# The first FFN matmul of segments 1 to 3 in 64-row tiles on a doubled input, with four general PSUM banks and a new timetable

## The chip, the core and the metric

The kernel runs on one core of a Trainium2 chip. Its engines each work through a queue of their own, in order, and wait for one another by semaphores: TensorE (PE, with PEld for its weight loads), VectorE (DVE), ScalarE (ACT), GpSimd (POOL) and SyncE (SP), whose queue issues nearly all DMAs. The metric is the device time of one execution in microseconds (us). The profile is taken in one further execution.

## The reference, cut to what matters

Two layers on a sequence of 2048 rows of 576 features, in bf16. The first is an attention with a memory, over four segments of 512 rows, the second a feed-forward network (FFN) of 4608 hidden features. Both have a layer norm ahead and a residual behind.

```python
# attention, per segment s of 4 (512 rows), 32 heads of 18
p = softmax(q @ k.T * scale + causal_mask);  a_dot = p @ v
a_mem = (phi(q) @ M) / (phi(q) @ z + 1e-6)      # M, z: sums over the segments ahead
o = g * a_mem + (1 - g) * a_dot
M += phi(k).T @ v;  z += phi(k).sum()
# the whole
h  = x + o @ wo                                  # q, k, v from layernorm(x)
h2 = h + gelu(layernorm(h) @ w1 + b1) @ w2 + b2  # w1: 576 x 4608, w2: 4608 x 576
```

## The kernel before, in words

The rows go through the core in four segments of 512 (s = 0 to 3, `L = 512`), each of four tiles of 128 rows (`TPS = 4`). The stages have letters, and the rows of the timetable begin with them: X (layer norm and transpose of the input), P (projections to q, k, v), M (the memory), A (attention), B (output projection, residual, second layer norm, transpose), C (first FFN matmul, called F1, with its Gelu) and D (second FFN matmul, F2, residual and output).

**Order.** Nothing is ordered by loops alone. `build()` lists operations (`add`), each with a cost per engine, the operations that it comes after, the buffers that it takes (`acq`) and those that it uses. The table `TIMETABLE` gives each one a letter for its engine (p, a, d, g, s) and a number, and `schedule()` sorts all operations by that number. So the order on every engine's queue is fixed in the table, ahead of the run. `schedule()` also picks for each buffer the slot that it expects to be free first; that is all that the costs are used for. The waits are set by the tile framework from reads and writes.

**PSUM.** There are eight banks of 512 fp32 columns. Three are general (`c_s`, tiles ps_c). One (`ox`) takes the value products of attention. The other four hold the scores (`st`, one buffer of four banks, in use from the first score step on), and after the last exp they become `ps_l`, four banks for F1 of segments 2 and 3 (`to_late`), which also uses `ox` then (`late_s`, five banks).

**F1 of segments 0 and 1** (L1224 and the lines around it). The normed rows lie transposed in `x2T`: features on the partitions, in five blocks of 128 (`KT = 5`), rows along the free axis. The 576 features fill four blocks and half of the fifth; the fifth block has a row of ones behind them, the 65th row (`KTAIL = 65`), which multiplies the bias b1. One block of 128 hidden features over 512 rows is five matmuls into one bank, and there are 36 such blocks (`NF = 36`); segment 0 does them in two halves of 256 rows. ACT or DVE copy the bank to `hT` (L597, L601), and in three batches a segment ACT does the Gelu in place (L1241), between the exps of attention; for each batch it loads the Gelu's table and then that of exp again. F1 of segment 1 stands among the score steps of attention of segments 2 and 3.

**F1 of segments 2 and 3** (L1188, `TILED = 2`) runs in 64-row tiles: TensorE works as two halves, rows 0 to 63 and 64 to 127, which each take a matmul at the same time, into banks of their own. The fifth block's upper half holds the last 64 features once more (`tail`, a copy on POOL, L1129), so that they can be had on either half. A group of four blocks is done in four phases of 5, 5, 4 and 4 pairs. In phases 0 and 1 a block takes its even chunks of 64 features on the lower half while another takes its odd chunks on the upper; in phases 2 and 3 the banks pass to the other half. Ahead of each passing stands a `mark`, a tiny memset on POOL (L1197) that waits for the phase that used the bank last. ACT does the Gelu with the bias straight from the bank (gelu1, L1208). This F1 can begin only after the last exp, when the score banks are free.

**x2T.** `flip` (L588) is a DMA transpose, issued on SP, from the rows in DRAM (`x2d`). The buffers xT (two, for the input of the projections) and x2T (one) are separate tiles; segments 1 and 3 put their transposed rows into an xT slot, segments 0 and 2 into the x2T slot. Segment 0's first half is transposed by TensorE.

**Weights.** A load on SP (L581) brings the weights of four blocks (640 KB) into one of three buffers `w1g`.

**Other lines.** L755 projections, L920 and L1049 scores (32-row tiles) of segment 0 and of the others, L924 and L1053 their exp, L945 and L1075 value products (32-column tiles in segments 1 to 3), L1027 the memory product ("mem") on exp of q (L1017, "eg"), L857 M, L1275 F2 (chunks of six matmuls of 288 columns), L1123 and L1287 the residuals.

Of the kernel before, what the change touches and what calls it, by code (L numbers as in the profile page):

```python
# [24 lines left out]
    "A00T": "p 166",  # L25
    "A00comb": "d 131 152",
    "A00copy": "d 171",
    "A00exp": "a 81 106",
    "A00mask": "g 95 103 133 128",
    "A00perm": "g 160",  # L30
    "A00st0": "p 76 96",
    "A00val": "p 105 129 145 147",
    "A01T": "p 224",
    "A01comb": "d 186 211",
    "A01copy": "d 227",
    "A01exp": "a 139 123 168 191",
    "A01mask": "g150 g165 d192 g190",
    "A01perm": "g 217",
    "A01st0": "p 136 118 151 187",
    "A01val": "p 163 179 169 167 197 199 205 208",  # L40
    "A02comb": "d 432 471",
    "A02dma": "s 487",
    "A02exp": "a 342 369 355 387 451 427",
    "A02mask": "g367 g351 d411 g398",
    "A02perm": "g 480",
    "A02st0": "p 339 364 353 382 446 408",
    "A02val": "p 378 394 380 390 393 410 436 437 468 463 457 449",
    "A03comb": "d 301 371",
    "A03dma": "s 460",
    "A03exp": "a 218 267 249 234 282 329 302 314",  # L50
    "A03flip": "s 503",
    "A03mask": "g 236 230 292 300",
    "A03opad": "g 585",
    "A03oxz": "d 484",
    "A03perm": "g 374",
    "A03st0": "p 214 264 246 231 279 325 295 309",
    "A03val": "p 248 260 285 281 263 266 258 257 313 316 366 341 336 315 334 333",
    "A0flip": "s 91 86 113 104 178 170 220 213",
    "A1comb": "d 579 624 663 719 757 794 829 847",
    "A1comb2": "g589 g636 d688 g722 d760 g803 g839 g851",  # L60
    "A1eg": "a 461 475 614 648 580 730 726 681",
    "A1exp": "a 469 499 483 550 515 570 587 604 620 634 657 671 693 707 734 721 763 776 792 808",
    "A1flip": "s 416 422 496 529 453 558 664 641",
    "A1mask": "g476 g507 d512 g516 g535 g565 g532 g527 g606 g610 g596 g615 g656 g650 g645 g660 d676 g680 d694 g701 g738 g735 d748 d746 g727 d782 d781 g789 "
        "g784 g820 g816 d838",
    "A1mem": "p 517 542 649 706 602 775 795 723",
    "A1memT": "d 521 549 655 709 607 779 815 737",
    "A1memfin": "d 525 631 677 712 704 798 835 828",
    "A1oT": "d 669 802 812 855 859",
    "A1pq": "d 500 492 643 697 584 755 765 710",  # L70
    "A1rg": "g 456 454 581 601 510 733 740 685",
    "A1st": "p 465 495 478 528 511 567 582 599 616 628 652 668 682 702 728 718 753 773 788 805",
    "A1val": "p 546 578 621 665 714 750 801 842",
    "A1valT": "d 561 598 659 689 744 790 809 845",
    "A2comb": "d 917 947 1003 1032 1059 1092 1128 1161",
    "A2comb2": "g922 g975 g1007 g1034 d1062 g1097 g1131 g1166",
    "A2eg": "a 804 874 878 968 1008 952 1056 1012",
    "A2exp": "a 849 823 869 883 899 915 944 930 961 973 987 1014 1028 1002 1044 1060 1074 1096 1087 1114",
    "A2flip": "s 767 800 824 787 898 868 1026 943",
    "A2mask": "g864 g830 g833 g880 g875 g893 d912 g908 g928 g953 d963 d937 d990 d969 d982 d986 d1000 g1023 g1020 d1036 d1046 g1029 g1061 g1052 g1069 g1103 "  # L80
        "g1081 d1106 g1129 d1120 g1127 g1121",
    "A2mem": "p 857 914 965 1009 1048 994 1072 1107",
    "A2memT": "d 863 927 974 1016 1050 997 1076 1110",
    "A2memfin": "d 865 971 1005 1021 1053 1030 1098 1112",
    "A2oT": "d 1070 1082 1155 1175 1179",
    "A2pq": "d 850 884 959 993 1033 983 1066 1088",
    "A2rg": "g 836 853 918 924 988 979 1064 1085",
    "A2st": "p 844 821 866 877 894 910 940 926 957 970 984 1010 1022 999 1038 1054 1071 1093 1083 1108",
    "A2val": "p 892 923 966 995 1040 1067 1111 1133",
    "A2valT": "d 902 931 980 1015 1045 1086 1116 1152",  # L90
    "A3comb": "d 1245 1273 1310 1362 1372 1399 1433 1443",
    "A3comb2": "g1261 g1276 g1329 d1366 g1379 g1403 d1437 d1444",
    "A3eg": "a 1119 1080 1229 1295 1268 1323 1383 1345",
    "A3exp": "a 1126 1139 1171 1186 1236 1257 1272 1219 1286 1301 1331 1313 1342 1351 1360 1374 1387 1397 1412 1426",
    "A3flip": "s 1041 989 1109 1115 1235 1164 1330 1284",
    "A3mask": "g1143 g1146 g1189 d1193 g1181 d1248 g1243 d1247 d1283 d1279 g1280 g1290 g1302 g1305 d1314 g1315 d1340 d1337 g1324 d1346 g1347 g1361 g1378 "
        "g1370 g1413 g1393 d1402 d1414 g1407 d1430 g1434 d1436",
    "A3mem": "p 1206 1228 1262 1316 1289 1380 1390 1416",
    "A3memT": "d 1210 1231 1265 1353 1303 1382 1405 1420",
    "A3memfin": "d 1259 1237 1288 1354 1306 1392 1424 1422",  # L100
    "A3oT": "d 1325 1455 1451 1445 1447",
    "A3pq": "d 1137 1144 1241 1308 1275 1376 1388 1350",
    "A3rg": "g 1100 1058 1140 1234 1253 1287 1384 1312",
    "A3st": "p 1122 1136 1162 1182 1230 1251 1270 1207 1282 1297 1326 1309 1339 1348 1357 1371 1385 1394 1408 1423",
    "A3val": "p 1209 1252 1294 1321 1349 1381 1421 1439",
    "A3valT": "d 1239 1269 1298 1334 1369 1395 1427 1441",
    "B00Po": "p 189 194",
    "B00T": "p 254",
    "B00apply": "d 232",
    "B00copy": "d 261",  # L110
    "B00dma": "s 143 524",
    "B00hadd": "d 196 200",
    "B00rstd": "g 223",
    "B00stats": "d 203",
    "B01Po": "p 233 237",
    "B01T": "p 262",
    "B01apply": "d 256",
    "B01copy": "d 265",
    "B01dma": "s 193 537",
    "B01hadd": "d 238 241",  # L120
    "B01rstd": "g 253",
    "B01stats": "d 244",
    "B02Po": "p 560 562",
    "B02apply": "d 609",
    "B02dma": "s 450 785 613",
    "B02hadd": "d 566 569",
    "B02rstd": "g 577",
    "B02stats": "d 572",
    "B03Po": "p 551 573",
    "B03apply": "d 627",  # L130
    "B03dma": "s 326 810 632",
    "B03flip": "s 651",
    "B03hadd": "d 556 576",
    "B03rstd": "g 622",
    "B03stats": "d 617",
    "B1Po": "p 897 901 867 881 872 873 933 938",
    "B1apply": "d 954 934 909 955",
    "B1dma": "s 886 951 956 818 996 936 807 887 913 905 962 960",
    "B1flip": "s 977",
    "B1hadd": "d 904 906 871 888 876 882 939 941",  # L140
    "B1rstd": "g 932 911 896 950",
    "B1stats": "d 920 895 891 945",
# [147 lines left out]
    "omg": "g 83",  # L290
    "ones": "a 278 338",
    "tri": "g 50",
    "warm": "p 5 11 18 23",
    "x1": "a 1",
}

# [1149 lines left out]
```

## Time and profile before

| what | value |
|---|---|
| time, median of 3 runs | 464.19 us (462.29 to 464.24) |
| the profiled execution: time | 463.85 us |
| the profiled execution: span, first to last instruction | 462.1 us |
| granted TensorE clock, mean | 0.996 |
| busy: PE, PEld, DVE, ACT, POOL | 451.1, 290.2, 288.7, 297.0, 143.3 us |
| F1 of segment 1 (L1224, 128x512) | 172 matmuls recorded, 41.2 us |
| F1 of segments 2 and 3 (L1188) | 324 pairs, from 309.0 to 426.3 us |
| F2 (L1275) | 1152 matmuls, 158.4 us |
| DMA | 78.10 MB, 169 GB/s in the mean |

How to read it: a group's row has its line, engine, operation and tile, then the busy time and mean duration in ns, then the engine's idle time ahead of it and what ended that. Matmuls overlap, so their mean duration is longer than the distance from one to the next; the timeline's starts give the distance. Some matmul records are missing, a few per cent. In a window's row, the first two numbers are the stretch and its length.

### The profile page before, as it was taken

The numbers are of one execution on the slowest core, as the hardware profiler recorded it, in microseconds if no ns is written. First come the engines' busy times: TensorE is split into PE (matmuls) and PEld (weight loads), VectorE is DVE, ScalarE is ACT, GpSimd is POOL, SyncE is SP. The second block draws the span as 40 slices with busy tenths as digits, with TensorE's granted clock in tenths as the row PEclk, the third lists the DMA queues.
The fourth block names the chain that finished last, engine by engine and source line by source line (L and its number), as shares of the span: only waits on it lengthen the run. The fifth ranks groups of instructions, "written<-read, shape, count | busy, mean of one in ns | idle before, by whom it ended". The sixth has DMA issues, their size and how long they took to land.

```text
span 462.1 us, 11032 instructions
## 1 busy us (share of the span) xinstructions
PE 451.1 (98%) x4569; PEld 290.2 (63%) x4577; DVE 288.7 (62%) x664; ACT 297.0 (64%) x283; POOL 143.3 (31%) x250
## 2 busy tenths in 40 slices
PE   8988999999999999999999999999999999999997
PEld 4766877866677776663344666554456774445775
DVE  6879978899987699889977887893211210000111
ACT  4877889999869787777899988744644004452100
POOL 4655415253513245445352244640001000001000
PEclk9989999999999999999999999999999999999999
DMA  7799789998798985555655125275650443351020
GB/s 242 221 270 208 227 278 293 230 264 235 224 238 280 326 218 147 160 119 128 198 167 147 39 64 146 70 192 165 199 205 16 112 165 112 129 177 43 8 75 22
DMA packets 75827, 78.10 MB, mean 169 GB/s; under 512 B 52992, under 2 KB 62976, under 8 KB 75776
## 3 DMA queue, kind: packets, MB, share of 16 engines
q1 hardware_dynamic: 75632, 77.24, 59.4%
q8 instruction: 36, 0.59, 0.5%
q10 hardware_dynamic: 144, 0.15, 0.1%
q14 instruction: 15, 0.12, 0.1%
HBM read 45.38 MB, written 19.53 MB: 140 GB/s over the span
## 4 chain that ended last, share of the span: by engine, by line
PE 81%; DVE 8%; ACT 4%; DMA 3%; SPq 2%; issue 1%; POOL 0%; DVEq 0%; ACTq 0%
PE ps_c L1275 28%; PE ps_c L1224 15%; PE ps_c L755 12%; PE ps_l L1188 11%; PE st L1049 4%; PE ox L1188 3%; PE ox L1075 3%; ACT pt L1053 2%; SPq L588 2%; ACT hT L1241 1%; PE ox L945 1%; PE ps_c L1027 1%; DMA xT<-xnd 1%; PE pr L766 1%; DMA qkd<-qk_pad 1%
## 5 line engine op out<-in xcount | busy, mean ns | idle before, releaser
L1275 PEld LDWEIGHTS <-hT 128*128 128x128 bf16 x1152 | 109.6, 98 | 37.8 <-issue 10.3
L1053 ACT ACTIVATE pt<-st 128x2048 bf16<-128x2048 f32 x60 | 112.7, 1878 | 30.4 <-PE st L1049 24.5
L1208 ACT ACTIVATE hT<-ps_l,b_col 128x512 bf16<-128x512 f32 x57 | 36.4, 687 | 66.7 <-PE ps_l L1188 64.4
L1275 PE MATMUL ps_c<-w,hT 128*128 128x288 bf16 x576 | 79.3, 287 | 0.0
L1275 PE MATMUL ps_c<-w_lo,hT 128*128 128x288 bf16 x576 | 79.1, 287 | 0.0
L1224 PEld LDWEIGHTS <-w1g 128*128 128x128 bf16 (+1 forms) x540 | 51.1, 97 | 26.1 <-issue 2.7
L755 PE MATMUL ps_c<-hT,xT 128*128 128x288 bf16 (+1 forms) x440 | 63.7, 290 | 1.9 <-DVE h L1123 1.1
L1064 POOL TENSOR_SCALAR_AFFINE_SELECT pt<-pt 128x512 bf16<-128x512 bf16 x63 | 42.6, 687 | 66.5 <-ACT pt L1053 66.4
L1287 DVE TENSOR_TENSOR ot<-ps_c,hc 128x288 bf16<-128x288 f32 x32 | 14.4, 451 | 75.0 <-PE ps_c L1275 46.4
L1188 PEld LDWEIGHTS <-w1g 64*128 64x128 bf16 x648 | 31.2, 94 | 37.9 <-issue 4.2
L755 PEld LDWEIGHTS <-xT 128*128 128x128 bf16 (+1 forms) x440 | 40.4, 98 | 15.2 <-issue 3.9
L601 DVE CAST hT<-ps_c 128x512 bf16<-128x512 f32 x51 | 34.7, 684 | 13.9 <-PE ps_c L1224 13.5
L1224 PE MATMUL ps_c<-x2T,w1g 128*128 128x256 bf16 (+1 forms) x360 | 43.2, 273 | 0.0
L924 ACT ACTIVATE pt<-st 128x2048 bf16<-128x2048 f32 x20 | 37.6, 1880 | 7.4 <-PE st L920 7.3
L1224 PE MATMUL ps_c<-xT,w1g 128*128 128x512 bf16 (+1 forms) x172 | 41.2, 380 | 0.4
L1188 PE MATMUL ps_l<-xT,w1g 64*128 64x512 bf16 x261 | 36.5, 377 | 0.3 <-ACT hT L1208 0.3
L1188 PE MATMUL ps_l<-x2T,w1g 64*128 64x512 bf16 x252 | 36.5, 377 | 0.0
L1197 POOL MEMSET mark<- 1x1 f32 x36 | 3.2, 88 | 99.1 <-PE ps_l L1188 85.5
L1241 ACT ACTIVATE hT<-hT 128x4608 bf16<-128x4608 bf16 (+2 forms) x7 | 32.1, 4592 | 0.1
L676 POOL TENSOR_TENSOR ln<-ln,mhalf 128x1 f32<-128x1 f32 x32 | 18.3, 576 | 37.4 <-DVE ln L673 37.3
L1123 DVE TENSOR_TENSOR h<-ps_c,xb 128x288 f32<-128x288 f32 x32 | 14.1, 452 | 24.6 <-PE ps_c L755 24.4
L1091 POOL TENSOR_TENSOR o_nat<-t,t 128x288 bf16<-128x288 f32 x18 | 16.9, 937 | 31.1 <-DVE t L1088 18.7
(116 smaller groups left out, 612.7 us busy)
## 6 DMA issues: line engine op xcount, KB each, us to landing
w1g<-in_B_w_dram SPq DMA_DIRECT2D x24, 640.0 KB, 4.7
w1g<-in_B_w1d_dram SPq DMA_DIRECT2D x18, 640.0 KB, 4.3
qkd<-qk_pad SPq DMA_DIRECT2D x15, 512.0 KB, 3.6
hd<-h SPq DMA_DIRECT2D x16, 288.0 KB, 3.3
hc<-hd SPq DMA_DIRECT2D x16, 288.0 KB, 3.2
w_lo<-in_B_w_dram SPq DMA_DIRECT2D x3, 864.0 KB, 5.2
w<-in_B_w_dram SPq DMA_DIRECT2D x3, 864.0 KB, 8.1
xb<-in_A_x_dram SPq DMA_DIRECT2D x16, 144.0 KB, 3.9
```

What stands on the lines that cost most here:

```text
L601: VEC[e].tensor_copy(out=dst(), in_=src())
L676: nc.gpsimd.tensor_tensor(out=sm.t[:, 15:16], in0=sm.t[:, 14:15], in1=mhalf[:], op=ALU.pow)
L755: nc.tensor.matmul(out=c.t[:, 0:HALF], lhsT=xTb.t[0:kk, k, ts], rhs=wt[0:kk, hf, k, :], start=(k == 0), stop=(k == 4))
L924: ex = add(ps, {"act": 1.88}, lambda e, st=st, pt=pt: nc.scalar.activation(out=pt.t[:], in_=st.t[:], func=ACT.Exp, scale=scale), [sc], pt, ...
L1049: nc.tensor.matmul(out=st.t[:, i, off:off + n_], lhsT=qk[rows, 1, kt * P:(kt + 1) * P], rhs=qk[rows, 0, kt * P:L], start=True, stop=True, ...
L1053: ex = add(ps, {"act": 1.88}, lambda e, st=st, pt=pt: nc.scalar.activation(out=pt.t[:], in_=st.t[:], func=ACT.Exp, scale=scale), [sc], pt, ...
L1064: nc.gpsimd.affine_select(out=blk, in_=blk, pattern=[[0, 4], [1, P]], compare_op=ALU.is_ge, fill=0.0, base=0, channel_multiplier=-1)
L1188: i = nc.tensor.matmul(out=cc[w].t[:], lhsT=w1.t[rows, ch // 2, w * P:(w + 1) * P], rhs=x2T[s].t[rows, ch // 2, :], start=ph < 2 and n == ...
L1208: ready_f[f] = [add(pf + 0.0001 * ph - 12, {"act": 0.68}, lambda e, f=f, w=w, cc=cc: nc.scalar.activation(out=hT[:, :, f, :], in_=cc[w].t[ ...
L1224: nc.tensor.matmul(out=c.t[:, u * n_:(u + 1) * n_], lhsT=w1.t[0:kk, k, j * P:(j + 1) * P], rhs=x2T[s].t[0:kk, k, ts], start=(k == 0), stop ...
L1241: ge = add(2.9 if half is None else GE_PRIO[half], {"act": (0.40 if half is None else 0.20) * (f1 - f0) + 0.25}, lambda e, f0=f0, f1=f1, h ...
L1275: nc.tensor.matmul(out=c.t[:, 0:HALF], lhsT=hT[:, tl // 2, f, (tl % 2) * P:(tl % 2 + 1) * P], rhs=w2_c[ch][:, f - ch * WCH, hf * HALF:(hf ...
```

## The change

- **Doubled input.** The tiles xT (two slots) and x2T become one tile `xreg`. For segments 1 to 3 its first nine blocks of 128 partitions are one buffer, `xd_s`, with nine blocks of two chunks each: the lower half holds the chunks 0 2 4 6 8 1 3 5 7, the upper half 1 3 5 7 0 2 4 6 8. Two flips fill it: the first as before (five blocks; the tail's 64 columns are now the first 64 features), the second four blocks from column 64 on. The first flip comes after all projections, since xT lies under it. There is one such buffer for three segments.
- **F1 of segments 1 to 3** does two blocks side by side: nine steps, each with a matmul on the lower half for one block and one on the upper half for the other. No bank passes from one half to the other, and the marks are gone. The weights are laid out to match (`by_pair`, 2304 columns a group in place of 2560) and are used for segment 1 too.
- **Segment 1** has no row of ones any more; the bias is added at the eviction (ACT Identity with a bias, or DVE add of a column). Its Gelu batches are 16, 14 and 6 blocks (15, 15 and 6 before). Segments 2 and 3 keep the Gelu from the bank.
- **Banks.** `ox` joins the general banks: four `c_s`, used for value products too; the late banks are four in place of five. The memset of ox is gone; the warm-up matmuls use general banks.
- **Planner.** Several costs are higher (flips, DVE operations); a flip's cost and size too.
- **Timetable.** Every row is new. A few are shown.

```diff
-    "A0flip": "s 91 86 113 104 178 170 220 213",
+    "A0flip": "s 96 85 127 119 184 192 202 231",
-    "B2flip": "s 1418",
+    "B2flip": "s 1360 1404",
-    "B3flip": "s 1618",
+    "B3flip": "s 1573 1584",
-    "C3F1": "p 1647 1648 1650 1652 1657 1660 1662 1664 1670 1672 1674 1676 1681 1684 1686 1688 1695 1696 1698 1700 1709 1712 1714 1716 1722 1727 1729 1731 "
-        "1754 1755 1757 1760 1736 1737 1741 1744",
+    "C3F1": "p 1612 1606 1620 1615 1627 1623 1630 1634 1641 1637 1648 1644 1655 1651 1658 1661 1667 1664",
...
-    BATCHES = (15, 30, 36)
-    TILED = 2
+    BATCHES = (16, 30, 36)
+    ND = 9
+    TILED = 1
+    DIRECT = 2
...
-    xT_s = slots(2, [P, KT, L], "xT")
-    x2_s = slots(1, [P, KT, L], "x2T")
+    xreg = const.tile([P, 3, KT, L], BF16, name="xreg")
+    xT_s = Slots([xreg[:, j, :, :] for j in range(2)])
+    x2_s = Slots([xreg[:, 2, :, :]])
+    xd_s = Slots([xreg[:].rearrange("p j k t -> p (j k) t")[:, 0:ND, :]])
...
-    ox_s = Slots([psum.tile([P, 512], F32, name="ox")])
-    c_s = slots(3, [P, 512], "ps_c", F32, psum)
+    c_s = slots(4, [P, 512], "ps_c", F32, psum)
...
-    late_s = Slots([None] * 4 + ox_s.tiles)
+    late_s = Slots([None] * 4)
...
-            x2T[s] = Buf(xT_s if s % 2 else x2_s)
+            x2T[s] = Buf(xd_s if s else x2_s)
...
                 if s >= TILED:
-                    ap = add(p0, {"pool": 0.2}, lambda e, xn2=xn2: nc.gpsimd.tensor_copy(out=xn2.t[:, D:XW], in_=xn2.t[:, D - 64:D]), [ap], None, [xn2],
+                    ap = add(p0, {"pool": 0.29}, lambda e, xn2=xn2: nc.gpsimd.tensor_copy(out=xn2.t[:, D:XW], in_=xn2.t[:, 0:64]), [ap] + first_ln, None, [xn2],
                              name="tail")
...
-                x2_ok[s].append(flip(prio, lambda: x2T[s].t[:], lambda: x2d[s][:, :], 520e3, w_, acq=x2T[s], cost=3.0))
+                x2_ok[s].append(flip(prio, lambda: x2T[s].t[:, 0:KT, :], lambda: x2d[s][:, :], 520e3, w_ + p3_done, acq=x2T[s], cost=3.0))
+                x2_ok[s].append(flip(prio, lambda: x2T[s].t[:, KT:ND, :], lambda: x2d[s][:, 64:D], 420e3, [x2_ok[s][0]], use=[x2T[s]], cost=2.4))
...
-                    if s >= TILED:
-
-                        cc = [Buf(late_s) for _ in range(4)]
-                        last, prev, phases, fences = {}, None, [], []
-                        pf = prh + 0.001 * (NF // 4 - fg)
-                        for ph in range(4):
...
+                    for q in (1, 0) if s >= TILED else ():
+                        f = fg * 4 + 2 * q
+                        cc = [Buf(c_s if s < DIRECT else late_s) for _ in range(2)]
+                        pf = prh + 0.001 * (NF - f)
+
+                        def fn(e, w1=w1, cc=cc, q=q):
+                            if s >= DIRECT:
+                                to_late()
+                            wv = w1.t[:].rearrange("p k f -> p (k f)")[:, 0:ND * 2 * P].rearrange("p (k q m) -> p k q m", q=2, m=P)
+                            for k in range(ND):
+                                for w in range(2):
+                                    rows = slice(64 * w, 64 * w + 64)
+                                    nc.tensor.matmul(out=cc[w].t[:], lhsT=wv[rows, k, q, :], rhs=x2T[s].t[rows, k, :], start=(k == 0), stop=(k == ND - 1))
+                        free = [o for w in range(2) for o in f2_chunks.get((s - 1, f + w), [])]
+                        a = add(pf, {"pe": 1.94}, fn, [la] + x2_in + free + (scores_done if s >= DIRECT else []), cc, [w1, x2T[s]], table="rows64", name="F1")
...
+                            def evict(e, f=f, w=w, cc=cc):
+                                dst, src, b = hT[:, :, f + w, :], cc[w].t[:].rearrange("p (h t) -> p h t", h=2), b1_col[:, f + w:f + w + 1]
+                                if e == "act":
+                                    nc.scalar.activation(out=dst, in_=src, func=ACT.Identity, bias=b)
+                                else:
+                                    nc.vector.tensor_scalar(out=dst, in0=src, scalar1=b, scalar2=None, op0=ALU.add)
+                            pend.append(add(pf - 16, {"act": 0.61, "dve": 0.69}, evict, [a, b1_ok], None, [cc[w]], name="copy"))
...
-                ox[g] = Buf(ox_s)
+                ox[g] = Buf(c_s)
...
+    def by_pair(w):
+        c = w.reshape(9, 64, 9, 2, 2, 128)
+        return np.concatenate([c[order, :, :, :, h].transpose(2, 1, 0, 3, 4) for h, order in enumerate(
+            ([0, 2, 4, 6, 8, 1, 3, 5, 7], [1, 3, 5, 7, 0, 2, 4, 6, 8]))], axis=1).reshape(9 * 128, 9 * 256)
...
-        B_w1d=by_group(blocks(w1, w1[512:576])),
+        B_w1d=by_pair(w1),
```

## The prediction

> **What bounds the kernel now.** I read the page's busy times first, then its 40 slices, then the windows by stage, the waits of TensorE, and the timeline where the first FFN matmul (F1) runs.
>
> ```profile
> span 462.1 us, 11032 instructions
> PE 451.1 (98%) x4569; PEld 290.2 (63%) x4577; DVE 288.7 (62%) x664; ACT 297.0 (64%) x283; POOL 143.3 (31%) x250
> PE   8988999999999999999999999999999999999997
> PEclk9989999999999999999999999999999999999999
> ...
> L1275 PE MATMUL ps_c<-w,hT 128*128 128x288 bf16 x576 | 79.3, 287 | 0.0
> L1208 ACT ACTIVATE hT<-ps_l,b_col 128x512 bf16<-128x512 f32 x57 | 36.4, 687 | 66.7 <-PE ps_l L1188 64.4
> ```
> TensorE (PE) is busy in every slice, and its clock is lower in one place only. F1's Gelu (L1208) waits 64 us for TensorE; nothing like that stands on the other side. After 50 us TensorE's waits on other engines add up to 2.1 us:
>
> ```profile
> PE ps_c L1027 <- DVE e L1021: 0.7, 2, 0.5
> PE st L1049 <- ACT pt L1053: 0.5, 2, 0.3
> PE ps_c L755 <- DVE oT L1100: 0.4, 1, 0.4
> PE ps_l L1188 <- ACT hT L1208: 0.3, 1, 0.3
> ```
> So from 50 us on the end is set by how many steps TensorE has to make. Two windows show where this is least sure: the start, and segment 3's attention, where ScalarE (ACT) is as full as TensorE.
>
> ```profile
> 28.00:32.00 4.00, 2.45 (x26) 1.57 (x27) 3.33 (x9) 1.83 (x6) 2.57 (x4) 0.79 1.07 314
> 32.00:36.00 4.00, 4.00 (x70) 3.17 (x69) 2.27 (x10) 2.93 (x5) 2.91 (x6) 0.79 1.16 283
> 205.00:309.00 104.00, 102.43 (x896) 56.22 (x905) 88.44 (x175) 87.10 (x57) 46.34 (x63) 1.00 0.45 125
> 245.00:265.00 20.00, 19.68 (x151) 11.72 (x152) 15.97 (x36) 19.52 (x12) 5.16 (x9) 1.00 0.30 86
> ```
> Columns: stretch, length, busy PE, PEld, DVE, ACT, POOL, granted clock, DMA share, GB/s. ACT is busy 19.52 of 20 us between 245 and 265.
>
> Prices of TensorE's steps come from the timeline (start, duration), from one start to the next:
>
> ```profile
> 234.07 7.75 PE L1224 MATMUL ps_c<-xT,w1g 128*128 128x512 bf16 x34
> 241.75 0.40 PE L1049 MATMUL st<-qk 32*128 32x256 bf16 x8
> 242.08 5.59 PE L1224 MATMUL ps_c<-xT,w1g 128*128 128x512 bf16 x24
> 247.60 0.40 PE L1049 MATMUL st<-qk 32*128 32x512 bf16 x4
> ...
> 375.42 1.63 PE L1275 MATMUL ps_c<-w_lo,hT 128*128 128x288 bf16 x12
> 376.89 1.64 PE L1275 MATMUL ps_c<-w,hT 128*128 128x288 bf16 x12
> ...
> 389.48 0.91 PE L1275 MATMUL ps_c<-w_lo,hT 128*128 128x288 bf16 x6
> 390.32 4.06 PE L1188 MATMUL ps_l<-xT,w1g 64*128 64x512 bf16 x36
> 394.32 0.91 PE L1275 MATMUL ps_c<-w,hT 128*128 128x288 bf16 x6
> ```
> Full-height F1: 35 matmuls (one record is missing) take 7.68 us and 25 take 5.52 us, so ten take 2.16: 0.216 each. Twelve F2 matmuls take 1.47, so a chunk of six 0.735. One chunk and 18 pairs of 64-row matmuls take 394.32 - 389.48 = 4.84. A pair at the full-height step of 0.216 makes 18 x 0.216 = 3.89; 4.84 - 0.735 - 3.89 = 0.22 is left for two changes of tile mode (128 rows to 64 and back): 0.11 each.
>
> **The change, part by part.** The sum is made against the profiled execution: 462.1 span, 463.85 time, 0.34 under the median of the three runs (464.19). Orders are those in which both kernels' instructions stand on each engine.
>
> *F1 of segment 1.* Now 36 blocks of 5 full-height matmuls, 180 x 0.216 = 38.9. After: 18 pairs of blocks of 9 steps, 162 x 0.216 = 35.0. TensorE: -3.9. Both halves of a step have the arrangement of L1188 (rows 0 to 63 and 64 to 127, a bank each). F1 of segments 2 and 3 has 162 steps before and after: nothing.
>
> The Trainium skill, "TensorEngine Tiling (Array Packing)", section "Instruction Overhead", speaks against this: it gives each matmul about 60 cycles of overhead, and segment 1 issues 324 instead of 180. Worked out from that page, an estimate, 144 x 25 ns = 3.6 us would eat this term and the forecast would be about 462.5. The row above has 36 matmuls in 18 steps of full-height length, so the row decides.
>
> *Changes of tile mode.* The orders have 221 before, 199 after: from segment 2's first F1 on 34 and 6 (16 of its 18 pairs, and all of segment 3's, now stand back to back), ahead of it 187 and 193, since segment 1's F1 has left the full mode. -22 x 0.11 = -2.4.
>
> *Segment 3's attention.* In the timeline a score step's exp starts 0.53 after the step (233.74, 234.27) and takes 1.88, and the scores have one buffer: the next step can start 2.43 after the last one. I filled the 19 gaps of the new order with rows: score step 0.33, F2 chunk 0.735, F1 pair 1.94, value product 0.55, memory product 0.12, 0.2 for changes of mode. Six gaps hold too little: a value and a memory product alone (short by 1.2), two chunks (0.4), two chunks and one or two memory products (0.3 and 0.2), one chunk with a value and a memory product (0.5, twice): 3.1. The old order gives 0.5 in the same way, which is what L1049 waited. Given back: +2.6. Behind a waiting score step stand the F2 chunks, which cannot pass it. Bounds: 0 (the exps still idle 24.5 us for scores over all segments) and +5.0, if the eight gaps that hold 2.5 to 2.75, and so just enough, are short by 0.3 each, half an exp of q (0.63, L1017; seven stand among these exps).
>
> *The start.* Before, TensorE waits 0.57 and 1.40 for flipped queries (L920), 0.58 for xT, 1.11 for h, and runs at 0.79 for 8 us, which is 1.7 us lost. After, the first two flips are issued ahead of a store of xn that they stood behind, two more half projections (0.62 each) stand ahead of the score step that waited first, and segment 0's memory product ahead of the other. That covers the 2.0; new are waits of values for masks and of a projection for its evacuated transpose, some 0.8 by the rows. I take -1.2. Bounds: -3.7 (2.0 and the half-speed stretch, 1.7) and +2.0 (a second such stretch and 0.3).
>
> The Trainium skill, "TensorE: Matmul & The Clock Gate", Part 1, says that the clock is halved after an idle window of about 3.4 us that runs free of the kernel. The two rows at 0.79 agree in size (1.7 us lost of 3.4); by the rule a stretch can come or go by phase alone, so the start could be worth 0 or -2.9 with the same order. The sum does not use it.
>
> *The doubled input.* Three more flips, of 4 blocks of 128 rows. A flip of 5 blocks holds SP 2.8 to 3.8 and lands 5 us after issue (L588, x2T and xT from x2d), so a second adds some 2.4 on SP's queue and 5 to readiness. There is one doubled buffer for three segments: a flip now waits for the last F1 of the segment ahead, and for the last projection of segment 3 (over by 130 us). What hides it: between the last F1 of segment 1 and the first of segment 2 stand some 40 F2 chunks (29 us), between those of 2 and 3 there are 48 (35 us). Behind the second flip on SP stand an output store, residual and weight loads, none needed within 10 us. Cost 0; without that cover about 10 us each. The added tail copy in segment 1 (POOL, 0.24, 4 of them) stands ahead of the same flip: 0.
>
> *Evictions.* In segment 1 the bias moves from the matmul's 65th row into 36 evictions, 25 on DVE and 11 on ACT. With a pointer operand ACT takes 0.687 (L1208) against 0.585 (L597), DVE 0.506 against 0.454 on 288 columns (L599, L601): 1.1 us on ACT, about 2.3 on DVE (0.052 scaled to 512 columns, 25 times), beside TensorE. DVE has 15 us free in 205 to 309. Cost 0 to 0.3, taken 0.
>
> *Banks, marks, loads.* F1 pairs take two of four banks. In segments 2 and 3 the two Gelus of a pair take 0.69 + 0.58 and the pair that runs meanwhile 1.94: not waited for. The 36 marks on POOL (L1197) and the memset of ox go: 0.2 us of waits, taken as 0. A weight group lasts 2 x 1.94 = 3.9 instead of 4.84; with three buffers the load is issued 7.8 ahead of use and lands in 4.3 (median), 6.6 at worst: 0.
>
> **Sum:** -3.9 - 2.4 + 2.6 - 1.2 = -4.9. 463.85 - 4.9 = 458.95; I say 459.0.
>
> **The rivals.**
> 1. *The start also loses its half-speed stretch:* waits 2.0 and clock 1.7 gone: -3.9 - 2.4 + 2.6 - 3.7 = -7.4, 456.4. For: fewer of the known waits meet in one place. Against: DMA is at 1.07 to 1.39 of its share there and every landing can slip.
> 2. *No measurable change:* attention gives back its upper bound and the start nothing: -3.9 - 2.4 + 5.0 = -1.3, 462.6. For: ACT at 29.0 of 30 us from 232 to 262. Against: 17 us of ACT's time are free in 205 to 309.
> 3. *Slower: ScalarE sets the pace of segment 3's attention.* Place: its score steps; price: an eviction or exp of about 0.6 inside the cycle of every one of 20 steps, +12.4 in place of 2.6: -3.9 - 2.4 + 12.4 - 1.2 = +4.9, 468.8. It decides from 0.5 us per step (9.8 cancel the rest plus 2.3). For: two Gelu batches (14 and 6 blocks; one of 15 takes 6.6) with their table loads (1.28 each) stand among the exps. Against: the old order has three there, and the new one only 2 evictions and 7 exps of q beside the 20 exps.
> 4. *The pairs do not run side by side in segment 1:* 324 x 0.216 = 70, some 490. L1188 excludes it but for a fault in the arrangement.
>
> **How the numbers follow.** Half a per cent is 2.3 us, about what a measurement can tell from no change. Forecast (457 to 461.5) 0.61, rival 1 0.17, rival 2 0.12, rival 3 0.09, rival 4 0.01. Faster: 0.61 + 0.17 = 0.78; same 0.12; slower 0.10. Of the bounds, all at once on the good side give 463.85 - 3.9 - 2.4 - 3.7 = 453.9, on the bad side 463.85 - 3.9 - 2.4 + 5.0 + 2.0 + 0.3 = 464.9; both need several to meet. 455.0 to 463.5 holds the forecast, most of rivals 1 and 2, and leaves out about 0.16. The forecast's own range is 457 to 461.5.
>
> **What would show it.** Right: F1 of segment 1 in pairs at 0.216 a step; from segment 2's first F1 to the end 3 us less (28 changes of mode); L1049 waiting for ACT about 3 us instead of 0.5; fewer waits of L920 for qkd. Wrong: TensorE waiting for a doubled flip or for weights ahead of F1; banks waited for in the back-to-back F1; a second stretch of low clock; the score steps of segment 3 at 2.4 us or more apart throughout with TensorE idle between.

## The result, and the profile after

| | before | after |
|---|---|---|
| median | 463.61 us (462.29 to 464.24, 4 runs) | 458.13 us (457.47 to 458.45, 4 runs) |
| profiled execution: time, span | 463.85, 462.1 us | 457.92, 456.2 us |
| granted TensorE clock in it | 0.996 | 1.000 |

The ratio is 0.988, with a 95% interval of 0.986 to 0.991: 5.5 us faster. 459.0 was predicted, 0.9 more than the median.

The page after, its busy times, two of its slices and the groups of F1 and of the evictions:

```profile
span 456.2 us, 11278 instructions
...
PE 443.6 (97%) x4721; PEld 290.2 (64%) x4721; DVE 282.5 (62%) x653; ACT 300.8 (66%) x285; POOL 148.6 (33%) x226
...
PE   7988999999999999999999999999999999999997
...
PEclk9999999999999999999999999999999999999999
...
L1192 ACT ACTIVATE hT<-ps_l,b_col 128x512 bf16<-128x512 f32 x72 | 45.2, 684 | 70.7 <-PE ps_l L1187 70.7
...
L1187 PE MATMUL ps_l<-xreg,w1g 64*128 64x512 bf16 x648 | 70.5, 376 | 0.0
...
L1187 PE MATMUL ps_c<-xreg,w1g 64*128 64x512 bf16 x324 | 37.2, 377 | 0.0
...
L1202 DVE TENSOR_SCALAR hT<-ps_c,b_col 128x512 bf16<-128x512 f32 x25 | 17.9, 743 | 6.9 <-PE ps_c L1187 6.7
```
PE is still busy in every slice, F1's Gelu still waits only for PE, and F1's own idle time is 0.0 in both groups: it waits neither for banks, nor for weights, nor for the doubled input. The digit of low clock has gone from PEclk; that is no work of the change alone, as shown below.

The windows after, the same stretches as before where the order allows it (columns: stretch, length, busy PE, PEld, DVE, ACT, POOL, granted clock, DMA share, GB/s):

```profile
205.00:309.00 104.00, 101.87 (x1058) 55.82 (x1057) 87.64 (x176) 87.61 (x59) 44.51 (x60) 1.00 0.51 124
...
245.00:265.00 20.00, 19.49 (x186) 11.41 (x184) 16.52 (x37) 19.63 (x12) 6.54 (x11) 1.00 0.49 139
28.00:32.00 4.00, 3.44 (x91) 2.89 (x91) 3.75 (x10) 2.19 (x4) 1.69 (x3) 1.00 0.81 241
32.00:36.00 4.00, 4.00 (x49) 2.98 (x47) 2.70 (x22) 3.57 (x6) 2.19 (x4) 1.00 0.66 163
```
ACT is as full between 245 and 265 as it was (19.63 of 20 us), and PE's busy time there is 0.2 less.

TensorE's waits after (engine, tile, line, what it waited for: total, times, longest):

```profile
PE st L1048 <- ACT pt L1052: 1.9, 5, 0.6
PE ps_c L856 <- DVE oq L958: 1.4, 1, 1.4
PE ps_c L609 <- DVE pt L603: 1.2, 1, 1.2
PE ps_c L754 <- DMA xreg<-xnd: 1.2, 1, 1.2
PE pr L765 <- DVE xreg L599: 0.6, 1, 0.6
PE pr L765 <- DMA hT<-in_A_w_dram: 0.5, 1, 0.5
...
PE ps_c L1026 <- ACT pt L1052: 0.4, 1, 0.4
PE ps_c L1074 <- DVE qk_pad L599: 0.3, 1, 0.3
PE ps_c L1074 <- DVE t L1029: 0.3, 1, 0.3
PE ps_c L1225 <- DMA w1g<-in_B_w_dram: 0.3, 1, 0.3
PE ps_c L1026 <- ACT hT L1200: 0.2, 1, 0.2
```
The wait for flipped queries (2.0 before) is gone; the scores wait 1.9 for the exp instead of 0.5, all of it in segment 3's attention. Of the two memory products (L1026) that wait for ACT, the one with 0.2 stands there too; the one with 0.4 stands in segment 1's attention, at 152.9 us.

The timeline after, where F1 of segment 1 begins, and a piece of segment 3's F1:

```profile
206.00 4.06 PE L1187 MATMUL ps_c<-xreg,w1g 64*128 64x512 bf16 x36
209.99 0.40 PE L1048 MATMUL st<-qk 32*128 32x384 bf16 x8
...
241.61 0.40 PE L1048 MATMUL st<-qk 32*128 32x384 bf16 x8 [0.58 <-ACT pt L1052]
...
383.65 16.57 PE L1187 MATMUL ps_l<-xreg,w1g 64*128 64x512 bf16 x152
```
In segment 1, 36 matmuls take 3.99 us from their start to the next step's; less about 0.1 for the change of mode that is 18 steps of 0.216. Segment 3's F1 stands in one run, with nothing between.

**Where the time went.** The trace gives every matmul's start. I added, for each kernel, the time from each matmul's start to the next one's by the step that it belongs to; idle time of TensorE counts to the step that waited:

| us | before | after | difference |
|---|---|---|---|
| start: warm-up, transposes, projections of segments 0 and 1, attention, memory and output projection of segment 0 | 67.25 | 65.53 | -1.72 |
| F1 of segment 1 | 40.01 | 36.58 | -3.43 |
| attention of segment 3 (scores, value and memory products) | 14.87 | 16.72 | +1.85 |
| F1 of segments 2 and 3 | 72.17 | 70.25 | -1.92 |
| other steps after segment 2's first F1 (F2, output projection) | 77.97 | 75.85 | -2.12 |
| everything else ahead of that F1 | 185.60 | 186.92 | +1.32 |
| sum | 457.87 | 451.84 | -6.02 |

The sum agrees with the two profiled executions (463.85 - 457.92 = 5.93). Segment 2's first F1 begins at 307.0 instead of 309.0; from there to the end of the span it is 149.2 instead of 153.2. Of "everything else", TensorE's idle time is 1.5 us after and 0.3 before: it is where new waits came up, in segment 1's attention and for weights (L1026, L1074, L1225 above).

### The profile page after: what moved, and what is told of

Its sections match the earlier page's. It is cut to its first block, busy times and chain, and to the rows that moved or that the text cites. A ratio compares the mean times of both kernels' runs of the same rounds, so it can differ in the third digit from the quotient of the medians.

```text
span 456.2 us, 11278 instructions
## 1 busy us (share of the span) xinstructions
PE 443.6 (97%) x4721; PEld 290.2 (64%) x4721; DVE 282.5 (62%) x653; ACT 300.8 (66%) x285; POOL 148.6 (33%) x226
## 4 chain that ended last, share of the span: by engine, by line
PE 83%; ACT 5%; DMA 5%; DVE 3%; SPq 1%; issue 1%; POOL 0%; ACTq 0%; DVEq 0%
PE ps_c L1276 30%; PE ps_l L1187 15%; PE ps_c L754 12%; PE ps_c L1225 8%; PE ps_c L1187 6%; PE st L1048 4%; ACT pt L1052 3%; PE ps_c L1074 2%; DMA w1g<-in_B_w_dram 1%; ACT hT L1207 1%; PE ps_c L944 1%; DMA hT<-in_A_w_dram 1%; DMA xreg<-xnd 1%; SPq L586 1%; PE ps_c L1026 1%
## 5 line engine op out<-in xcount | busy, mean ns | idle before, releaser
L1187 PEld LDWEIGHTS <-w1g 64*128 64x128 bf16 x972 | 46.7, 94 | 57.1 <-issue 3.3
L1187 PE MATMUL ps_l<-xreg,w1g 64*128 64x512 bf16 x648 | 70.5, 376 | 0.0
L754 PE MATMUL ps_c<-hT,xreg 128*128 128x288 bf16 (+1 forms) x440 | 61.2, 286 | 1.3 <-DMA xreg<-xnd 1.2
L754 PEld LDWEIGHTS <-xreg 128*128 128x128 bf16 (+1 forms) x440 | 40.5, 97 | 13.9 <-issue 1.9
L1225 PE MATMUL ps_c<-xreg,w1g 128*128 128x256 bf16 (+1 forms) x360 | 43.6, 272 | 0.3 <-DMA w1g<-in_B_w_dram 0.3
L1225 PEld LDWEIGHTS <-w1g 128*128 128x128 bf16 (+1 forms) x360 | 34.0, 97 | 6.8 <-issue 1.1
L1187 PE MATMUL ps_c<-xreg,w1g 64*128 64x512 bf16 x324 | 37.2, 377 | 0.0
L1048 PE MATMUL st<-qk 32*128 32x512 bf16 (+3 forms) x384 | 23.8, 300 | 1.9 <-ACT pt L1052 1.9
L1202 DVE TENSOR_SCALAR hT<-ps_c,b_col 128x512 bf16<-128x512 f32 x25 | 17.9, 743 | 6.9 <-PE ps_c L1187 6.7
L754 PE MATMUL ps_c<-wt_o,oT 128*128 128x288 bf16 x160 | 22.1, 286 | 0.0
```

Source lines behind the costliest of these rows:

```text
L754: nc.tensor.matmul(out=c.t[:, 0:HALF], lhsT=xTb.t[0:kk, k, ts], rhs=wt[0:kk, hf, k, :], start=(k == 0), stop=(k == 4))
L1048: nc.tensor.matmul(out=st.t[:, i, off:off + n_], lhsT=qk[rows, 1, kt * P:(kt + 1) * P], rhs=qk[rows, 0, kt * P:L], start=True, stop=True, ...
L1187: nc.tensor.matmul(out=cc[w].t[:], lhsT=wv[rows, k, q, :], rhs=x2T[s].t[rows, k, :], start=(k == 0), stop=(k == ND - 1))
L1202: nc.vector.tensor_scalar(out=dst, in0=src, scalar1=b, scalar2=None, op0=ALU.add)
L1225: nc.tensor.matmul(out=c.t[:, u * n_:(u + 1) * n_], lhsT=w1.t[0:kk, k, j * P:(j + 1) * P], rhs=x2T[s].t[0:kk, k, ts], start=(k == 0), stop ...
```

## The experiments

The comparisons are with the kernel before on the same chip. Its median there is 463.18 for the second series of the changed kernel, the price of a change with its control, and segment 1 at full height; 463.95 for the variant of that with 65 rows and for the flip doubled in segments 2 and 3 only; 463.21 for the other four. The ratios are to these medians' runs.

### The changed kernel again

> The changed kernel itself, for comparison on this chip. Theory (fewer TensorE steps and fewer mode changes): 458.0, between 457.3 and 458.7, a ratio of 0.988. If the start's half-speed stretch of the clock were worth its 1.7 us, executions with a mean clock of 0.995 would be 1.7 us longer than those at 1.000; the four executions so far do not show that (0.995: 458.34 and 457.47; 1.000: 457.92 and 458.45), so I expect no difference.

Measured: 458.46 us (457.26 to 459.5, 6 runs), ratio 0.989 (0.987 to 0.991). Its profiled execution has a span of 457.8 instead of 456.2, and the table above gives the reason: every row but the start agrees to 0.2, the start has 66.91 instead of 65.53. The windows of the start of this execution (busy PE, granted clock, DMA share, GB/s), those of the other one below:

```profile
30.00:34.00 4.00, 3.86 (x76) 0.65 0.58 159
32.00:36.00 4.00, 4.00 (x46) 0.68 0.96 186
```

```profile
30.00:34.00 4.00, 4.00 (x86) 1.00 0.87 267
32.00:36.00 4.00, 4.00 (x49) 1.00 0.66 163
```
The same program, in the same order, has a stretch of low clock there in one execution and not in the other. Its mean clock tells which: the changed kernel's ten runs have a median of 457.91 without it (4 runs, clock 1.000) and 458.68 with it (6, 0.995 to 0.996), the 44 runs of before 462.74 without (24) and 464.01 with it (20). The ranges overlap; the stretch costs about 1 us, against none that was expected here, and the gain is 4.8 without it and 5.3 with it. So the change did not remove it; the two profiles that the result compares happened to differ in it. Six of this case's twelve traces have the stretch. In each of them it lasts 3.41 us at half the clock, begins between 28.6 and 31.2 us, and stands 7 or 8 times 3.41 us after the clock first rose.

### The price of a change of tile mode

```diff
+                            if s == 3:
+                                nc.tensor.matmul(out=cc[0].t[:, 0:64], lhsT=ident[:], rhs=ident[:, 0:64], start=True, stop=True)
                             for k in range(ND):
```


> In segment 3 a matmul of 64 columns in full mode ahead of each of the 18 pairs of F1, into the bank that the pair clears next. Theory (a change of mode costs 0.11): 17 more round trips, 34 x 0.11 = 3.7, and 18 x 0.03 for the matmuls: +4.2 us over the changed kernel, between +3.4 and +5. Rival (mode changes cost nothing; the end of the kernel became shorter because the marks and the passing of banks are gone): +0.5, like the control.

Measured: 461.92 us (460.09 to 463.28, 12 runs), ratio 0.997 (0.9955 to 0.9987), 3.5 us over the changed kernel's 458.46. The control keeps the added columns and leaves the mode alone:

```diff
+                            if s == 3:
+                                for w in range(2):
+                                    rows = slice(64 * w, 64 * w + 64)
+                                    nc.tensor.matmul(out=cc[w].t[:, 0:64], lhsT=ident[rows, :], rhs=ident[rows, 0:64], start=True, stop=True)
                             for k in range(ND):
```


> Control of the run before: two matmuls of 64 columns in 64-row mode, one on each half, ahead of each of segment 3's 18 pairs, so that no mode changes. Both theories: 18 x 0.03 = +0.5 us over the changed kernel, between +0.2 and +1.

Measured: 458.24 us (457.53 to 459.25, 5 runs), ratio 0.989 (0.987 to 0.991). The two timelines, first the one with the full-height matmul:

```profile
386.29 0.20 PE L1185 MATMUL ps_l<-ident 128*128 128x64 bf16 x1
386.42 2.12 PE L1189 MATMUL ps_l<-xreg,w1g 64*128 64x512 bf16 x18
388.47 0.20 PE L1185 MATMUL ps_l<-ident 128*128 128x64 bf16 x1
```

```profile
385.60 0.19 PE L1187 MATMUL ps_l<-ident 64*128 64x64 bf16 x2
385.62 2.11 PE L1191 MATMUL ps_l<-xreg,w1g 64*128 64x512 bf16 x18
387.57 0.19 PE L1187 MATMUL ps_l<-ident 64*128 64x64 bf16 x2
```
One pair with its small matmul takes 2.18 us in the first and 1.97 in the second: 0.21 for two changes. Segment 3's F1 takes 39.29 us against 35.60; 3.69 over 34 changes is 0.109 each. In the medians it is 3.68 us. The price that the prediction used (0.11) holds. A pair of small matmuls in the control costs 0.03: (35.60 - 35.07) / 18, with 35.07 for the changed kernel's F1 of segment 3.

### Segment 1 at full height again

```diff
+                            if s < DIRECT:
+                                for w in range(2):
+                                    j = 2 * q + w
+                                    for k in range(KT):
+                                        kk = 64 if k == 4 else P
+                                        nc.tensor.matmul(out=cc[w].t[:], lhsT=w1.t[0:kk, k, j * P:(j + 1) * P], rhs=x2T[s].t[0:kk, k, :],
+                                                         start=(k == 0), stop=(k == KT - 1))
+                                return
```
(with the weights in the old layout for segment 1)

> F1 of segment 1 at full height again (10 steps for two blocks in place of 9 pairs), all else as in the changed kernel. Step theory: 18 more steps of 0.216, +3.9, less 5 changes of mode of 0.11 (199 to 194), so +3.3 us over the changed kernel, between +2.5 and +3.9: about 461.4. Rival (ScalarE sets the pace among the score steps, so that steps saved in segment 1 are given back there): +0 to +1, below 459.2.

Measured: 466.25 us (465.67 to 467.86, 6 runs), ratio 1.007 (1.005 to 1.009): more than twice what was expected, and slower than before. Segment 1's F1 takes 46.35 us. A piece of its timeline, and its groups with shapes kept apart:

```profile
223.95 5.22 PE L1188 MATMUL ps_c<-xreg,w1g 128*128 128x512 bf16 x20
229.10 0.40 PE L1048 MATMUL st<-qk 32*128 32x256 bf16 x8
```

```profile
L1188 PE MATMUL ps_c<-xreg,w1g 128*128 128x512 bf16 x144 | 37.3, 382 | 0.0
...
L1188 PE MATMUL ps_c<-xreg,w1g 64*128 64x512 bf16 x36 | 13.9, 387 | 0.0
```
Twenty matmuls take 5.15 us to the score step's start; at 0.216 they would take 4.32 and a change of mode. The fifth matmul of each block has exactly 64 rows. If it runs in the 64-row mode, four blocks have seven changes more (the last one would be there anyway): 7 x 0.11 = 0.77. The kernel before did not have this, since its row of ones made the fifth matmul 65 rows high. The test of that reading is one number:

```diff
-                                        kk = 64 if k == 4 else P
+                                        kk = KTAIL if k == 4 else P
```


> The changed kernel with F1 of segment 1 at full height again, as in the run before with that edit, but with the fifth matmul of each block on 65 rows instead of 64. Reading of that earlier run: its fifth matmul of exactly 64 rows ran in the 64-row tile mode, so each of the 36 blocks paid two changes of mode (ten matmuls 2.64 us instead of 2.16; 36 x 0.225 = 8.1). Theory: with 65 rows the block goes back to 5 x 0.216, and F1 of segment 1 costs 180 x 0.216 = 38.9 against 35.0 of the changed kernel, less some 1.4 for changes of mode that the full height does not have around each visit: +2.5 over the changed kernel, about 461 (460 to 462.3), ten matmuls 2.16 us. Rival: the loss of the earlier run came from something else than the tile mode of the fifth matmul (the doubled input's layout, the order of the work): about 466 again, ten matmuls 2.6 us. What the kernel computes changes: the 65th row of segment 1's block adds b1 times the first feature.

Measured: 460.30 us (459.64 to 462.06, 6 runs), ratio 0.992 (0.9895 to 0.9945).

```profile
223.41 4.51 PE L1188 MATMUL ps_c<-xreg,w1g 128*128 128x512 bf16 x20
227.84 0.40 PE L1048 MATMUL st<-qk 32*128 32x256 bf16 x8
```
The 20 matmuls now take 4.43, 0.72 less, and segment 1's F1 39.92 instead of 46.35: 6.43, or 63 changes (two for each of 36 blocks, less one at the end of each of nine visits, where a score or value step brings a change anyway) at 0.10. The median is 2.2 us over the changed kernel's 458.13 (1.4 to 1.7 by the ratios to the kernel before on each chip). One row more makes this variant some 6 us faster. So F1 of segment 1 in pairs is worth 39.92 - 36.58 = 3.3 us on TensorE. The Trainium skill, "TensorEngine Tiling (Array Packing)", section "Key Properties", says that a switch of the tiling mode drains TensorE; it gives no time for it, and the runs put 0.10 to 0.11 us on each.

### The evictions with a bias

```diff
-                                    nc.scalar.activation(out=dst, in_=src, func=ACT.Identity, bias=b)
+                                    nc.scalar.copy(out=dst, in_=src)
...
-                                    nc.vector.tensor_scalar(out=dst, in0=src, scalar1=b, scalar2=None, op0=ALU.add)
+                                    nc.vector.tensor_copy(out=dst, in_=src)
```


> Segment 1's evictions are plain copies again, without the bias (its b1 is left out). DVE 25 x 0.05 and ScalarE 11 x 0.1 less. Theory (beside TensorE): 0, between -0.4 and 0.1 us against the changed kernel. Rival (evictions hold back banks or exps): -1 to -3.

Measured: 458.13 us (456.64 to 458.78, 6 runs), ratio 0.988 (0.985 to 0.990): no difference from the changed kernel (458.13 and 458.46) that the medians can tell. The evictions are hidden, as said.

### ScalarE's share in segment 3's attention

```diff
-                                out=hT[:, :, f0:f1, :], in_=hT[:, :, f0:f1, :], func=ACT.Gelu_apprx_tanh), pend, table="gelu", name="gelu")
+                                out=hT[:, :, f0:f0 + 1, :], in_=hT[:, :, f0:f0 + 1, :], func=ACT.Gelu_apprx_tanh), pend, table="gelu", name="gelu")
```


> The three Gelu batches of segment 1 do one block each instead of 16, 14 and 6 (their table loads stay), so segment 1's hidden features mostly miss their Gelu. ScalarE has 33 x 0.42 = 14 us less to do among segment 3's score steps. Theory (the give-back there is ScalarE's): TensorE's waits for ScalarE (1.9 of score steps, 0.6 of memory products) go, -1.5 to -2.5 us against the changed kernel, about 456. Rival (those gaps are short for other reasons, or VectorE is next): 0 to -0.5.

Measured: 457.25 us (457.13 to 458.64, 6 runs), ratio 0.987 (0.985 to 0.9895): 0.9 to 1.2 us under the changed kernel's two medians; the intervals overlap, and the trace tells more. Segment 3's attention takes 15.77 us on TensorE instead of 16.72. Of the waits, one line is of use here; below it, from the changed kernel, ACT around the second Gelu batch and the score step behind it:

```profile
PE st L1048 <- ACT pt L1052: 1.3, 4, 0.5
```

```profile
250.09 6.18 ACT L1207 ACTIVATE hT<-hT 128x7168 bf16<-128x7168 bf16 x1
...
257.58 1.88 ACT L1052 ACTIVATE pt<-st 128x2048 bf16<-128x2048 f32 x1
```

```profile
259.50 0.40 PE L1048 MATMUL st<-qk 32*128 32x384 bf16 x8 [0.51 <-ACT pt L1052]
```
With some 14 us of ACT's work taken out of segment 1's Gelu, the scores still wait 1.3 of 1.9 us. So most of the wait is not a busy ACT: it is the distance of two score steps over one buffer (0.53 to the exp and 1.88 for it) where the gap holds too little work. The changed kernel's trace says the same: four of its five waits, 1.4 us, stand behind an exp that began 0.44 to 0.53 us after its score step, the shortest delay that exps have in that stretch. The fifth, 0.51 at 259.5, stands behind an exp that a Gelu batch held back until 8.2 us after its score step (249.38), and it is the one that is gone in this run. The 0.9 us of TensorE's time that the run did gain is what the Gelu batches delay: this wait, 0.2 at a memory product and 0.1 at the first wait are 0.8 of it.

### The second flip issued twice

```diff
+                once = x2_ok[s][-1].fn
+
+                def twice(e, once=once):
+                    once(e)
+                    once(e)
+                x2_ok[s][-1].fn = twice
```


> The second flip of each doubled input is issued twice (same data): three more DMA transposes, 2.4 us each on the queue of SyncE and some 4.5 us to landing. Theory (hidden by F2 chunks): 0, within 0.5 us of the changed kernel. Rival (the flip is on the path, or delays the weights queued behind it): +2.4 to +7 a segment, +5 us or more.

Measured: 460.93 us (457.45 to 463.02, 11 runs), ratio 0.994 (0.991 to 0.996), some 2.5 us over the changed kernel: the expectation fell. In its trace TensorE waits for the doubled input, in one place; the line of the waits, and the timelines there, of SP's queue and of TensorE:

```profile
PE ps_c L1193 <- DMA xreg<-x2d: 1.6, 1, 1.6
```

```profile
198.75 9.10 SPq L586 DMA_TRANSPOSE xreg<-x2d  x2
```

```profile
207.23 1.25 PE L1193 MATMUL ps_c<-xreg,w1g 64*128 64x512 bf16 x10
210.11 2.12 PE L1193 MATMUL ps_c<-xreg,w1g 64*128 64x512 bf16 x18 [1.62 <-DMA xreg<-x2d]
```
That is segment 1: the repeat leaves the queue at 207.9 and lands at 210.1. F1 does its first five pairs on the blocks of the first flip and waits with the sixth. In the changed kernel the second flip is issued at 197.35, holds the queue for 3.29 and lands at 204.3, and F1's first pair starts at 206.00:

```profile
197.35 3.29 SPq L586 DMA_TRANSPOSE xreg<-x2d  x1
201.07 6.29 SPq L586 DMA_TRANSPOSE qk<-qkd  x2
```
So 1.7 us are left to the first pair, and 2.8 to the sixth. The next run doubles the flip where the prediction had named its cover, in segments 2 and 3 only:

```diff
-                x2_ok[s][-1].fn = twice
+                if s > 1:
+                    x2_ok[s][-1].fn = twice
```


> The changed kernel with the second doubled flip issued twice for segments 2 and 3 only. The earlier run had it twice in all three segments and lost 2.2 us at the median, and its trace has TensorE waiting 1.6 us for segment 1's doubled input and nothing at segments 2 and 3. Theory: the cover is thin in segment 1 alone (in the changed kernel its second flip leaves the queue at 200.6 and the first F1 pair of segment 1 stands at 205.7; the 29 and 35 us of F2 chunks that the prediction named lie ahead of segments 2 and 3), so the time is that of the changed kernel, 458.2 (457.3 to 459.2), and TensorE waits for no doubled input. Rival: any further flip costs time, by its DMA traffic or by what stands behind it on SP: 459.5 to 461.

Measured: 457.83 us (457.06 to 459.29, 5 runs), ratio 0.987 (0.985 to 0.9895): nothing lost, and no wait of TensorE's matmuls for a doubled input. But segment 2 is not as well covered as was expected; SP's queue and TensorE there:

```profile
297.17 7.21 SPq L586 DMA_TRANSPOSE xreg<-x2d  x2
```

```profile
306.72 2.55 PE L1194 MATMUL ps_l<-xreg,w1g 64*128 64x512 bf16 x22
```
The repeat lands at 306.5, 0.3 us ahead of the first pair. In the changed kernel segment 2's second flip lands at 302.9, 4.1 us ahead of its F1, and segment 3's 12.8 us ahead. Of the 2.5 us of the run before, F1 of segment 1 accounts for 1.8 (38.38 instead of 36.58 in the table's terms, the wait of 1.6 in it); the rest is not placed.

### The old F1 in one run

The kernel before, with the F2 chunks of segments 2 and 3 moved out of segment 3's F1, so that it has 16 changes of mode fewer (205 instead of 221):

```diff
-    "D2F2": "p 1601 ... 1636 1646 1654 1678 1690 1702 1707 1569 ... 1645 1666 1718 1733",
+    "D2F2": "p 1601 ... 1636 1646 1646.1 1646.3 1646.4 1646.5 1646.6 1569 ... 1645 1646.2 1646.7 1646.8",
-    "D3F2": "p 1748 1753 1765 ... 1771 1746 1750 1761 ...
+    "D3F2": "p 1760.2 1760.4 1765 ... 1771 1760.1 1760.3 1761 ...
```


> The kernel before, with F1 of segment 3 in one run: the 8 F2 chunks of segment 2 that stood among it go ahead of it, the 4 of segment 3 behind it. 221 changes of mode become 205. Theory (0.11 each): -1.8 us against the kernel before, ratio 0.996, between 0.9945 and 0.998. Rival (the four-phase F1 needs the chunks between, for its marks and its banks to come free): no gain, or +0.5 to +2.

Measured: 466.87 us (465.62 to 467.8, 6 runs), ratio 1.007 (1.004 to 1.009), 3.7 us slower instead of 1.8 faster. Segment 3's F1 takes 39.26 us, where before it took 36.21. Its waits in that stretch:

```profile
its engine sat idle before it (us, times) until:
  ACT hT L1208: 1.5, 4
  DMA w1g<-in_B_w1d_dram: 0.5, 1
```
In the old form a bank passes between the halves and a group of weights is used up faster once no F2 chunk stands between, so F1 waits for Gelus (0.3 before) and for weights. These 2.0 us are named by the trace; another 2 by which its steps are longer than 0.216 are small gaps between phases for which it names no one. From segment 2's first F1 to the end the run takes 155.3 us, 2.1 more than before, although 16 changes are gone; the other 1.1 of the two profiles' difference stands ahead of that, where the edit changes no order, most of it in the start. The F2 chunks between the phases, which cost two changes of mode each, were paying for the waits that they hid. Pairs that keep their banks can stand back to back; the old phases could not.

## Why the prediction was right

459.0 was predicted by a sum of four terms, -4.9 in all; the profiles differ by 5.9 and the medians by 5.5. The likeliest case came true, with its terms off in both directions, so that the nearness of the sum is in part luck:

| step | predicted | measured |
|---|---|---|
| F1 of segment 1, 180 steps to 162 | -3.9 | -3.4 on TensorE with its own changes of mode in it; -3.3 against the same kernel at full height with 65 rows |
| changes of mode, from segment 2's first F1 on | -3.1 | some -3.0 (28 at 0.10 to 0.11) of the -4.0 to the end of the span |
| changes of mode ahead of it | +0.7 | not measured by itself; part of F1 of segment 1, of attention and of everything else |
| segment 3's attention | +2.6 | +1.9; waits for ACT 2.1 against 0.5 |
| start | -1.2 | -1.7 between the profiles; -0.3 where both have the low clock |
| doubled flips | 0 | 0, with less cover than was named |
| evictions | 0 | 0 |
| banks, marks, loads | 0 | -0.3 (a wait for a Gelu), inside the -4.0 |
| waits between the start and segment 3's attention | not in the sum | +1.2 (1.5 against 0.3) |

*Steps and modes.* Both prices were read from starts in the trace of before, and both held: 0.216 for a pair of half-height matmuls, 0.10 to 0.11 for a change of mode. The overhead per matmul that the Trainium skill states ("TensorEngine Tiling (Array Packing)", section "Instruction Overhead"), 3.6 us here by the prediction's estimate, does not appear as an addition: segment 1's 324 matmuls run in 162 steps of full-height length.

*The tail.* From segment 2's first F1 on, 28 changes explain 2.8 to 3.1 of 4.0. Another 0.7 is idle time of TensorE that the old trace has in this stretch and the new one has not: 0.3 for a Gelu, which "Banks, marks, loads" took as 0, and 0.4 at the output projection (L755, for oT). Some 0.3 is not placed. No matmul waits for a mark or for weights there before (one weight load waits 0.2 for a mark); the run of the old F1 without chunks shows that this form is close to such waits.

*Attention.* Gaps filled with rows gave +2.6. By TensorE's account it is +1.9, and by its waits for ACT +1.6: scores 1.9 and a memory product 0.2 against 0.5. The mechanism was the one named, oversized: four of the five waits are of that kind, 1.4 us, where the short gaps had added up to 3.1, and with ACT relieved of 14 us the scores still wait 1.3. The fifth, 0.5, is a busy ACT. Rival 3 (ScalarE in every cycle) is excluded: five of twenty score steps waited, 0.6 at most.

*The start.* Right in number, not in cause. The waits for flipped queries went, as said (2.0 to none), and the one for h (1.1), but a new wait for DVE (L856, 1.4), a longer one for a flipped input (L754, 1.2 instead of 0.6) and two of the projections for an eviction and weights (L765, 0.6 and 0.5) took the place of both: TensorE's idle time in the start's steps, after its first matmul, is 4.6 us instead of 4.3. What shortened the start in the profile is the missing stretch of low clock (3.41 us at half the clock, 1.7 lost), which rival 1 had counted as an effect of the change. The Trainium skill ("TensorE: Matmul & The Clock Gate", Part 1), which the prediction weighed and set aside, has the window behind such a stretch run free of the kernel (3.4 us long there, and the stretches of the traces are 3.41), from which the prediction drew that a stretch can come or go by phase alone; two executions of one program differ in it here. Like for like the start is worth little, and the account then is -3.43 - 4.04 + 1.85 - 0.35 + 1.52 = -4.45 (the last term is everything else in that execution's account), beside the 4.35 by which its time of 459.5 lies under 463.85.

*What the sum left out.* Outside the start it charged no new waits ahead of segment 3's attention. The trace has 1.2 us more of them, of value and memory products of segment 1's attention for DVE and ACT, and for weights of segment 0's F1. They come to about what the tail gained beyond its changes of mode.

*The flips.* The prediction named F2 chunks of 29 and 35 us as cover. A second flip too many costs nothing in segments 2 and 3, but the flips are issued late in that cover, so that 4.1 and 12.8 us are left, not 29 and 35. For segment 1 no cover was named, and there it is 1.7 us. The conclusion held, the argument had a hole.

## What to carry to other kernels

Read a change of TensorE's tile mode as a step with a price (0.10 to 0.11 us here) and count the changes in the order of instructions: a K tail of 64 rows in a full-height accumulation is such a change twice, and one padded row avoids it. Work put between two phases can be what hides their waits, so before taking it out look at what the phases wait for with it; a form that passes no banks is what allowed the long runs here. Compare two profiles by stage and clock before a difference at the start is credited to the change: a stretch of low clock moved this one by 1.4 us with the same program. And read a transfer's cover from its landing to its use, not from the work that stands between two uses of its buffer.

## What was not expected of the hardware

- A matmul of exactly 64 rows among 128-row ones costs 0.20 us more (two changes of mode), one of 65 rows nothing: 466.25 us against 460.30 for one row in 36 matmuls.
- The stretch of low clock in the first 40 us is there in some executions and not in others: by the mean clock in 6 of 10 runs of the changed kernel and 20 of 44 of the one before, about 1 us each.
- Two matmuls of 64 columns side by side cost 0.03 us, about an eighth of the 0.216 of two with 512: at this size no fixed cost per matmul shows.
